# State sums and results inside a chunk as one product, on one core

## The chip, the cores and the metric

The kernel runs on one core of a Trainium2 chip. The metric is the device time of one execution in microseconds. TensorE (PE) multiplies, VectorE (DVE), ScalarE (ACT) and GpSimd (POOL) do the elementwise work, and SyncE (SP) issues nearly all transfers. In the profile PEld stands for the weight loads of TensorE, which run beside its products.

## What is computed

An mLSTM cell over 4 batches x 8 heads, 768 steps, head size 40, and then a SwiGLU block on its 3072 x 320 output with 1536 hidden columns:

```
for t in range(S):
    m_new = maximum(f[t] + m, i[t])
    C = exp(f[t] + m - m_new) * C + exp(i[t] - m_new) * outer(v[t], k[t])
    n = exp(f[t] + m - m_new) * n + exp(i[t] - m_new) * k[t]
    y[t] = sigmoid(o[t]) * (C @ q[t]) / maximum(abs(n @ q[t]), 1)
x = y as (tokens, 320)
out = (silu(x @ w_gate) * (x @ w_val)) @ w_out
```

## The kernel before

**Tiling.** The sequence is cut into six chunks of 128 tokens for all 32 heads, and each chunk into two subchunks of 64 (index i), which lie on partitions 0 to 63 and 64 to 127. Heads are taken in pairs (index two), 16 pairs in all, and the pairs in two groups P of eight (index a). All products are f32. Inside a subchunk the recurrence becomes matrices: scores of keys and queries (`scores`, L309) times exponential weights `w_sb` (`weigh`, L316) give a 64 x 64 matrix per head; its product with the values gives the results inside the subchunk (`intra`, L354). What came earlier is held in a state per subchunk (`C_ring`, three buffers, 41 columns, the last of which carries n), and recalled by a product with the queries (`inter`, L349). The state advances by a decay (POOL, L339) and by the sum of keys times weighted values (`add`, L330; DVE, L341). The weighted values `vw_sb` are made by `weigh_values` (L319).

**On TensorE** each of `scores`, `add`, `inter` and `intra` is 32 matmuls for one group and chunk, 64 rows by 64 columns of stationary operand, issued so that the four follow each other on the four quarters of the array. The profile shows two passes per f32 matmul, each with its own weight load.

**Gathering.** `gather` scales the recalled part (L364), adds the part inside the chunk in four pieces of 64 partitions (L371) and makes the denominator (L373 to L375). `gate` multiplies by the sigmoid of the output gate (L380), `divide` writes `x_sb` (L385), and `seam` transposes it into `xT` (L400), the input of the SwiGLU block.

**The SwiGLU block** for a group g of 512 tokens (128 of each batch) is `hidden(g, m)` for twelve m: 10 matmuls of 64 x 128 stationary and 512 moving columns (L546), Silu on ACT (L551), the product on DVE into `h_sb` (L552); then `project` (L562) or, for group 0, `project_all` (L569).

**Order.** It is written out by hand. While hidden(g, m) runs for group g, the cell work of chunk g + 1 is put between its products by a table of slots, one after each m. The engines run their queues in this order. PSUM has four banks under the tag "cell", handed out in turn to all cell products and transposes, and four under "gen" for the hidden products and the projections. The first chunk is worked ahead of everything, with burns (idle products, L430) between its steps. Meanwhile the weights, which arrive as 64-bit floats, are loaded in pieces (L157) and turned into f32 by `scale` on ACT (L182, L184), `join` on DVE (L192, L193) and `rounded` on POOL or DVE (L200). The stabilizer rows `M_sb` of the later chunks are written to DRAM (L283), and come back spread over 64 partitions as `w_sb` (L408), are subtracted (L412), masked (L417) and exponentiated (L421).

Of the kernel before, what the change touches and what calls it, by code (L numbers as in the profile page):

```python
# [24 lines left out]
def kernel(  # L25
# [55 lines left out]
    def heads(P):  # L81
        return slice(P * UH, (P + 1) * UH)
# [5 lines left out]
    w_sb = const.tile([128, BH, SUB], F32)  # L88
    vw_sb = const.tile([128, BH, D1], F32)
# [23 lines left out]
    def copy(eng, dst, src):  # L113
        if eng is nc.scalar:
            nc.scalar.copy(dst, src)
        else:
            eng.tensor_copy(dst, src)

# [100 lines left out]
    junk = early.tile([128, 512], BF16)  # L219
# [19 lines left out]
    nc.gpsimd.memset(C_ring[0], 0.0)  # L239
# [12 lines left out]
    M_sb = early.tile([BH, NS - 2, SUB], F32)  # L252
# [24 lines left out]
    def late_maxima():  # L277
        nc.vector.tensor_tensor_scan(flat(M_sb), flat(step1), flat(i_sb), M0[0:BH, 1, last], op0=ALU.add, op1=ALU.max)
        nc.vector.tensor_add(m_in[:, 0:1], M0[0:BH, 1:2, last], f0[0:BH, 1:2, last])
        nc.vector.tensor_add(m_in[:, 1:], M_sb[:, 0:NL - 1, last], f_sb[:, 0:NL - 1, last])  # L280
        nc.vector.tensor_sub(step1, m_in.to_broadcast([BH, NL, SUB]), M_sb)
        nc.scalar.activation(step1, step1, AF.Exp)
        nc.sync.dma_start(out=M_dram, in_=flat(M_sb))  # L283

    M_dram = tc.dram_tile([BH, S - L], F32, name="M_dram")
# [27 lines left out]
    def weigh(P, sp):  # L313
        w2 = w_sb[:, heads(P)].rearrange("p (a two) t -> p two a t", two=2)
        for two in range(2):
            nc.vector.tensor_tensor(w2[:, two], sp[two], w2[:, two], op=ALU.mult)  # L316

    def weigh_values(eng, P):
        eng.tensor_tensor(vw_sb[:, heads(P)], v_sb[:, heads(P)], w_sb[:, heads(P), last].to_broadcast([128, UH, D1]),  # L319
                          op=ALU.mult)  # L320
# [3 lines left out]

    def add(P):
        ps = [small("add") for _ in range(2)]
        for a in range(UA):
            for i, two in QUAD:
                h = P * UH + 2 * a + two
                nc.tensor.matmul(ps[i][half(two), a, :], lhsT=k_sb[half(i), h, :], rhs=vw_sb[half(i), h, :],  # L330
                                 start=True, stop=True)
        return ps
# [4 lines left out]
    def next_state(s, P, ps):  # L337
        a = slice(P * UA, (P + 1) * UA)
        nc.gpsimd.tensor_tensor(state(s + 1)[:, a], state(s)[:, a],  # L339
                                dec[:, s - 1, a].unsqueeze(2).to_broadcast([128, UA, D1]), op=ALU.mult)  # L340
        nc.vector.tensor_tensor(state(s + 1)[:, a], state(s + 1)[:, a], ps, op=ALU.add)  # L341


    def attend(n, P):
        inter = [small("inter") for _ in range(2)]
        intra = [small("intra") for _ in range(2)]
        for a in range(UA):
            for two, i in QUAD:
                nc.tensor.matmul(inter[two][half(i), a, :], lhsT=qT[half(two), P * UA + a, half(i)],  # L349
                                 rhs=state(2 * n + i)[half(two), P * UA + a, :], start=True, stop=True)  # L350
        for a in range(UA):
            for i, c in QUAD:
                h = P * UH + 2 * a + (i ^ c)
                nc.tensor.matmul(intra[i][half(c), a, :], lhsT=w_sb[half(i), h, :], rhs=v_sb[half(i), h, :],  # L354
                                 start=True, stop=True)
        return inter, intra

    def gather(n, P, inter, intra):
        y = work.tile([128, UH, D1], F32, name="y_sb")
        y2 = y.rearrange("p (a two) d -> p two a d", two=2)  # L360
        e2 = e_T[:, n, heads(P)].rearrange("p (a two) -> p two a", two=2)
        own = slice(SUB, 128) if n == 0 else slice(0, 128)
        for two in range(2):
            nc.vector.tensor_tensor(y2[own, two], inter[two][own],  # L364
                                    e2[own, two].unsqueeze(2).to_broadcast([own.stop - own.start, UA, D1]), op=ALU.mult)
        for i, c in QUAD:
            t = y2[half(i), i ^ c]
            if n == 0 and i == 0:
                nc.scalar.copy(t, intra[i][half(c)])
            else:  # L370
                nc.vector.tensor_tensor(t, t, intra[i][half(c)], op=ALU.add)  # L371
        den = work.tile([128, UH, 1], F32, name="den")
        nc.vector.scalar_tensor_tensor(den, in0=y[:, :, D:], scalar=-1.0, in1=y[:, :, D:], op0=ALU.mult, op1=ALU.max)  # L373
        nc.vector.tensor_scalar(den, den, scalar1=1.0, scalar2=None, op0=ALU.max)
        nc.vector.reciprocal(den, den)  # L375
        return y, den
# [28 lines left out]
    def weights_load(n):  # L405
        for i in range(2):
            src = M_dram[:, ds((n - 1) * L + i * SUB, SUB)].unsqueeze(0).to_broadcast([SUB, BH, SUB])
            nc.sync.dma_start(out=w_sb[half(i)], in_=src)  # L408

    def weights_sub(n, P):  # L410
        gb = g_T[:, n, heads(P)].unsqueeze(2).to_broadcast([128, UH, SUB])
        nc.vector.tensor_tensor(w_sb[:, heads(P)], gb, w_sb[:, heads(P)], op=ALU.subtract)  # L412

    def weights_mask(P):
        for i in range(2):
            w = w_sb[half(i), heads(P)]
            nc.gpsimd.affine_select(w, w, compare_op=ALU.is_ge, fill=NEG, base=0, pattern=[[0, UH], [1, SUB]],  # L417
                                    channel_multiplier=-1)

    def weights_exp(P):  # L420
        nc.scalar.activation(w_sb[:, heads(P)], w_sb[:, heads(P)], AF.Exp)  # L421
# [5 lines left out]
    def burn(n):  # L427
        t = bank("burn")
        for _ in range(n):
            nc.tensor.matmul(t, lhsT=junk[:, 0:128], rhs=junk, start=True, stop=True)  # L430
# [22 lines left out]
    def first_weights(P):  # L453
        for u in (2 * P, 2 * P + 1):
            nc.scalar.activation(w_sb[:, u * H:(u + 1) * H], wps[u], AF.Exp)
# [3 lines left out]
    def first_sums(P):  # L459
        ps = add(P)  # L460
        for i in range(2):
            nc.scalar.copy(state(i + 1)[:, P * UA:(P + 1) * UA], ps[i])
# [5 lines left out]
    weigh_values(V, 0)  # L468
    sp = scores(0)
    weigh(0, sp)  # L470
    first_sums(0)
# [4 lines left out]
    burn(2)  # L476
    at = attend(0, 0)
    weigh_values(G, 1)
    y0, den0 = gather(0, 0, *at)
# [6 lines left out]
    first_sums(1)  # L486
# [3 lines left out]
    at = attend(0, 1)  # L490
    y1, den1 = gather(0, 1, *at)
# [93 lines left out]
    def do_add():  # L585
        for P in range(2):
            live["add", P] = add(P)

    def do_state(s, P):
        for i, ps in enumerate(live.pop(("add", P))):  # L590
            next_state(s + i, P, ps)

    def do_attend(n, P):
        live["at", P] = attend(n, P)

    def do_gather(n, P, then=True):
        live["y", P] = gather(n, P, *live.pop(("at", P)))
        if then:
            do_gate(P)

    def do_gate(P):
        gate(P, live["y", P][0], nc.gpsimd)

    def do_divide(P):
        divide(P, live.pop(("y", P))[1])

    def load_all(dst, a, n):
        for P in range(2):
# [16 lines left out]
            run(weigh_values, G, 0), run(weigh_values, G, 1), run(piece_load, 8)],  # L625
        9: [run(do_scores), run(do_weigh, 0), run(load_all, o_sb, o_gate, 1)],
        10: [run(do_weigh, 1), run(do_add), run(do_state, 2, 0), run(do_state, 2, 1), run(piece_load, 9)],
        11: [run(do_attend, 1, 0), run(do_gather, 1, 0, False)],
    }
    piece_load(4)  # L630
    for m in range(NFC):
# [4 lines left out]
        0: [run(do_attend, 1, 1), run(convert, 14), run(sig, 0), run(sig, 1), run(do_gate, 0)],  # L636
# [14 lines left out]
    weigh_values(G, 0)  # L651
    weigh_values(G, 1)
# [5 lines left out]
    for g in range(1, NG):  # L658
        n, f = g + 1, g + 2
        slots = {m: [] for m in range(NFC)}  # L660
        if n < NG:
            slots[0] = [run(turn, 0, (A, V), (A, V))]
            slots[1] = [run(turn, 1, (A, V), (A, V))]
            slots[3] = [run(do_scores), run(do_weigh, 0)]
            slots[4] = [run(do_weigh, 1)]
            slots[5] = [run(do_add), run(do_state, 2 * n, 0)]
            slots[6] = [run(do_state, 2 * n, 1)]
            slots[7] = [run(do_attend, n, 0), run(do_gather, n, 0)]
            slots[8] = [run(do_divide, 0)]
            slots[9] = [run(do_attend, n, 1), run(do_gather, n, 1)]  # L670
            slots[10] = [run(do_divide, 1), run(seam, n, 0, (A, V, A, V))]
            slots[11] = [run(seam, n, 1, (A, V, A, V))]
# [9 lines left out]
        for u in range(B):  # L682
# [3 lines left out]
            if f < NG and u == 2:  # L686
                weights_exp(0)
                weights_exp(1)
                sig(0)
                sig(1)  # L690
                weigh_values(nc.gpsimd, 0)
                weigh_values(nc.gpsimd, 1)
# [31 lines left out]
```

## Time and profile before

| | us |
|---|---|
| median of 3 runs | 589.06 (589.0 to 589.62) |
| profiled execution | 589.0, of which the span is 587.2 |
| first hidden product (L546) starts | 45.6 |
| from one group's first hidden product to the next (groups 2, 3, 4) | 90.1 |
| TensorE busy | 564.7 (96% of the span) |
| DVE, ACT, POOL busy | 210.0, 152.0, 101.9 |

The span runs from the first to the last instruction. Up to 45.6 us TensorE is busy for 30.8 us with the first chunk, its transposes and the burns, while the DMA engines are 99% busy. From there to 143 us group 0 runs, with the DMA engines at 89%; from 165 to 506 us TensorE is busy without a gap, and DMA is below a half.

### The profile page before, as it was taken

What the parts mean: (1) busy time and instruction counts of PE and PEld (TensorE: products, weight loads), DVE (VectorE), ACT (ScalarE), POOL (GpSimd) and SP (SyncE); (2) the same over time, 40 slices, a digit from 0 to 9 for tenths busy, and PEclk for the clock granted to TensorE, in tenths of its full rate; (3) what the DMA queues carried; (4) which work ended last, traced back from release to release, by engine and by line L of the source; (5) the groups of instructions that cost most, each with busy time, mean ns of one, the idle gap of its engine ahead of it and who ended that gap; (6) DMA issues with size and microseconds to landing.
All of it is one profiled execution on the core that took longest, in us unless ns stands there. A gap on an engine that the chain in (4) does not pass through costs nothing.

```text
span 587.2 us, 13173 instructions
## 1 busy us (share of the span) xinstructions
PE 564.7 (96%) x5904; PEld 326.2 (56%) x5904; DVE 210.0 (36%) x376; ACT 152.0 (26%) x242; POOL 101.9 (17%) x102
## 2 busy tenths in 40 slices
PE   7759998999999999999999999999999999999997
PEld 4534454676555567555567554567555557544475
DVE  6445666683224630233740223650133550011100
ACT  3437455432601114311014310114211110011100
POOL 2103524455201232001232001133001110000000
PEclk9879999999999999999999999999999999999999
DMA  9999893599304450303360114180000000000000
GB/s 127 180 192 154 169 219 101 129 152 137 55 1 58 80 85 22 57 2 47 61 114 23 35 23 47 32 132 28 18 2 2 2 2 23 22 1 0 1 21 24
DMA packets 129919, 37.91 MB, mean 65 GB/s; under 512 B 120424, under 2 KB 125032, under 8 KB 129864
## 3 DMA queue, kind: packets, MB, share of 16 engines
q1 hardware_dynamic: 129636, 36.85, 36.5%
q8 instruction: 46, 0.75, 0.6%
q10 hardware_dynamic: 228, 0.23, 0.2%
q14 instruction: 9, 0.07, 0.0%
HBM read 33.06 MB, written 4.01 MB: 63 GB/s over the span
## 4 chain that ended last, share of the span: by engine, by line
PE 80%; ACT 1%; DVE 1%; DMA 0%; issue 0%; ACTq 0%; DVEq 0%
PE gv_ps L546 45%; PE o_ps L562 22%; PE o_ps L569 4%; PE inter L349 2%; PE intra L354 2%; PE add L330 2%; PE sp L309 1%; PE tp_kq L294 1%; PE tp_x L400 1%; ACT w_sb L421 0%; DMA out_dram<-z_sb 0%; ACT o_sb L424 0%; ACT L551 0%; ACT L424 0%; ACT L421 0%
## 5 line engine op out<-in xcount | busy, mean ns | idle before, releaser
L546 PE MATMUL gv_ps<-xT,wgv_sb 64*128 64x512 f32 x1440 | 321.7, 594 | 3.6 <-DVE wgv_sb L200 2.6
L546 PEld LDWEIGHTS gv_ps<-xT,wgv_sb 64*128 64x128 f32 x1440 | 138.1, 187 | 158.5 <-issue 151.2
L552 DVE TENSOR_TENSOR h_sb<-sg,gv_ps 128x512 f32<-128x512 f32 x72 | 49.5, 687 | 300.7 <-ACT sg L551 283.8
L562 PE MATMUL o_ps<-wo_sb,h_sb 128*128 128x320 f32 x480 | 130.5, 433 | 0.0
L551 ACT ACTIVATE sg<-gv_ps 128x512 f32<-128x512 f32 x72 | 43.0, 598 | 269.4 <-PE gv_ps L546 269.3
L562 PEld LDWEIGHTS o_ps<-wo_sb,h_sb 128*128 128x128 f32 x480 | 90.8, 190 | 38.2 <-issue 0.8
L339 POOL TENSOR_TENSOR C<-C,dec 128x328 f32<-128x328 f32 x20 | 14.5, 737 | 165.1 <-DVE C L341 165.1
L556 ACT COPY z_sb<-o_ps 128x320 f32<-128x320 f32 x24 | 10.2, 426 | 114.1 <-PE o_ps L562 102.7
L417 POOL TENSOR_SCALAR_AFFINE_SELECT w_sb<-w_sb 64x1024 f32<-64x1024 f32 x20 | 26.8, 1338 | 28.8 <-DVE w_sb L412 27.9
L569 PE MATMUL o_ps<-wo_sb,h_sb 128*128 128x320 f32 x96 | 26.9, 437 | 0.0
L371 DVE TENSOR_TENSOR y_sb<-y_sb,intra 64x328 f32<-64x328 f32 x44 | 21.7, 493 | 7.9 <-PE intra L354 6.9
L380 POOL TENSOR_TENSOR o_sb<-o_sb,y_sb 128x640 f32<-128x640 f32 x10 | 14.2, 1426 | 48.3 <-DVE y_sb L371 48.3
L569 PEld LDWEIGHTS o_ps<-wo_sb,h_sb 128*128 128x128 f32 x96 | 17.9, 190 | 7.2
L319 POOL TENSOR_TENSOR vw_sb<-v_sb,w_sb 128x656 f32<-128x656 f32 x11 | 14.1, 1304 | 39.4 <-issue 29.3
L354 PE MATMUL intra<-v_sb,w_sb 64*64 64x41 f32 x768 | 14.5, 229 | 6.4 <-issue 6.4
L349 PEld LDWEIGHTS inter<-C,qT 64*64 64x64 f32 x768 | 12.5, 134 | 9.0 <-issue 7.8
L330 PEld LDWEIGHTS add<-vw_sb,k_sb 64*64 64x64 f32 x768 | 13.2, 141 | 6.9 <-issue 5.7
L354 PEld LDWEIGHTS intra<-v_sb,w_sb 64*64 64x64 f32 x768 | 13.3, 136 | 6.4 <-issue 6.4
L330 PE MATMUL add<-vw_sb,k_sb 64*64 64x41 f32 x768 | 14.2, 233 | 2.7 <-issue 1.4
L316 DVE TENSOR_TENSOR w_sb<-sp,w_sb 128x512 f32<-128x512 f32 x24 | 15.4, 683 | 2.3 <-PE sp L309 2.2
L200 POOL TENSOR_TENSOR wgv_sb<-both,low 128x640 int32<-128x640 int32 x8 | 12.3, 1542 | 21.3 <-DVE both L193 21.3
L193 DVE SCALAR_TENSOR_TENSOR both<-top,both 128x640 uint32<-128x640 uint32 x18 | 15.7, 870 | 0.6
(111 smaller groups left out, 358.7 us busy)
## 6 DMA issues: line engine op xcount, KB each, us to landing
w_sb<-M_dram SPq DMA_DIRECT2D x10, 512.0 KB, 6.4
k_sb<-in_k_dram SPq DMA_DIRECT2D x12, 320.0 KB, 6.6
q_sb<-in_q_dram SPq DMA_DIRECT2D x12, 320.0 KB, 4.1
v_sb<-in_v_dram SPq DMA_DIRECT2D x12, 320.0 KB, 5.5
o_sb<-in_o_gate_dram SPq DMA_DIRECT2D x12, 320.0 KB, 6.9
raw<-in_moe_w_out_dram SPq DMA_DIRECT2D x3, 1280.0 KB, 6.0
out_dram<-z_sb SPq DMA_DIRECT2D x24, 160.0 KB, 1.8
raw<-in_moe_w_gate_dram SPq DMA_DIRECT2D x3, 640.0 KB, 6.6
```

Source lines behind the costliest of these rows:

```text
L193: nc.vector.scalar_tensor_tensor(both, in0=top, scalar=0x80000000, in1=both, op0=ALU.bitwise_and, op1=ALU.bitwise_or)
L316: nc.vector.tensor_tensor(w2[:, two], sp[two], w2[:, two], op=ALU.mult)
L330: nc.tensor.matmul(ps[i][half(two), a, :], lhsT=k_sb[half(i), h, :], rhs=vw_sb[half(i), h, :], start=True, stop=True)
L349: nc.tensor.matmul(inter[two][half(i), a, :], lhsT=qT[half(two), P * UA + a, half(i)], rhs=state(2 * n + i)[half(two), P * UA + a, :], sta ...
L354: nc.tensor.matmul(intra[i][half(c), a, :], lhsT=w_sb[half(i), h, :], rhs=v_sb[half(i), h, :], start=True, stop=True)
L371: nc.vector.tensor_tensor(t, t, intra[i][half(c)], op=ALU.add)
L417: nc.gpsimd.affine_select(w, w, compare_op=ALU.is_ge, fill=NEG, base=0, pattern=[[0, UH], [1, SUB]], channel_multiplier=-1)
L546: nc.tensor.matmul(ps[i], lhsT=wgv_sb[half(i), PAIRS[kc][i], ts(m, 128)], rhs=x[half(i), kc, :], start=(kc == 0), stop=(kc == NKC - 1))
L551: nc.scalar.activation(sg, ps[0], AF.Silu)
L552: nc.vector.tensor_tensor(hid(g, m), sg, ps[1], op=ALU.mult)
L562: nc.tensor.matmul(p, lhsT=hid(g, m)[:, ts(u, L)], rhs=wo_sb[:, m, :], start=(m == 0), stop=(m == NFC - 1))
L569: nc.tensor.matmul(ps[u], lhsT=hid(g, m)[:, ts(u, L)], rhs=wo_sb[:, m, :], start=(m == 0), stop=(m == NFC - 1))
```

## The change

The weights `w_sb` and new weighted keys `kw_sb` become parts of one tile `wk_sb`, four parts of 64 columns per pair of heads in the order weighted keys 0, weights 0, weights 1, weighted keys 1. `add` now takes two neighbouring parts as one stationary operand of 128 columns, with the plain values as the moving operand; one product gives the state sum of a head on one half of the partitions and its results inside the chunk on the other. The `intra` products go. A product for one group now uses four banks instead of two.

Around it:

- `weigh_keys` takes the place of `weigh_values` (keys of 40 columns instead of values of 41); its zero columns are set once at the start.
- `own_results` copies the results from PSUM into `y_sb`, in four pieces of 64 partitions: on DVE in the first chunk, on ACT later. `next_state` adds in two pieces of 64 partitions per subchunk instead of one of 128.
- `gather` scales the recalled part into the places of `w_sb` that are no longer needed, and adds it to `y_sb` in one operation over 656 columns.
- `recall` leaves out the product with the zero state in chunk 0. In later chunks both groups' recalls stand together in slot 8 (before in slots 7 and 9), with both gathers; `add` of the two groups stands in slots 5 and 6 (before both in 5), the first divide in slot 9. In chunk 1 `add` stands in slots 10 and 11, and both recalls come after the first step of `project_all` (L569).
- `M_dram` is laid out by pairs, so that a row of it holds two heads: the load of `w_sb` has runs of 512 bytes (before 256), the store two transfers with runs of 256 bytes (before one, 2560).
- One call of two burns is left out in the first chunk, `M_sb` shares the buffer of `f_sb`, and the burns' operand is smaller.

```
-    w_sb = const.tile([128, BH, SUB], F32)
-    vw_sb = const.tile([128, BH, D1], F32)
+    wk_sb = const.tile([128, PP, 4, SUB], F32)
...
+    w_sb = wk_sb[:, :, 1:3, :]
+    kw_sb = wk_sb[:, :, 0:4:3, :]
...
+    def weigh_keys(eng, P):
+        eng.tensor_tensor(kw_sb[:, pairs(P), :, 0:D], by_two(k_sb[:, heads(P), 0:D]),
+                          w_sb[:, pairs(P), :, last].to_broadcast([128, UA, 2, D]), op=ALU.mult)
...
     def add(P):
-        ps = [small("add") for _ in range(2)]
-        for a in range(UA):
-            for i, two in QUAD:
-                h = P * UH + 2 * a + two
-                nc.tensor.matmul(ps[i][half(two), a, :], lhsT=k_sb[half(i), h, :], rhs=vw_sb[half(i), h, :],
-                                 start=True, stop=True)
+        ps = [[small("add") for _ in range(2)] for _ in range(2)]
+        for two in range(2):
+            for a in range(UA):
+                for i in range(2):
+                    nc.tensor.matmul(ps[two][i][:, a, :],
+                                     lhsT=wk_sb[half(i), P * UA + a, 2 * two:2 * two + 2, :].rearrange("p x t -> p (x t)"),
+                                     rhs=v_sb[half(i), P * UH + 2 * a + two, :], start=True, stop=True)
         return ps
...
-    def next_state(s, P, ps):
...
+    def next_state(s, P, ps, i):
+        a = pairs(P)
+        new = state(s + 1)
+        nc.gpsimd.tensor_tensor(new[:, a], state(s)[:, a], dec[:, s - 1, a].unsqueeze(2).to_broadcast([128, UA, D1]),
+                                op=ALU.mult)
+        for two in range(2):
+            t = new[half(two), a]
+            nc.vector.tensor_tensor(t, t, ps[two][i][half(two)], op=ALU.add)
+
+    def own_results(ps, engs):
+        y = work.tile([128, UH, D1], F32, name="y_sb")
+        for two in range(2):
+            for i in range(2):
+                copy(engs[i], by_two(y)[half(i), :, two], ps[two][i][half(1 - two)])
+        return y
+
+    def recall(n, P):
...
+                if n or i:
+                    nc.tensor.matmul(inter[two][half(i), a, :], lhsT=qT[half(two), P * UA + a, half(i)],
+                                     rhs=state(2 * n + i)[half(two), P * UA + a, :], start=True, stop=True)
...
+    def gather(n, P, y, inter):
...
+        t = w_sb[own, pairs(P), :, 0:D1]
         for two in range(2):
+            nc.vector.tensor_tensor(t[:, :, two], inter[two][own],
+                                    e2[own, :, two].to_broadcast([own.stop - own.start, UA, D1]), op=ALU.mult)
+        nc.vector.tensor_tensor(by_two(y)[own], by_two(y)[own], t, op=ALU.add)
...
-    burn(2)
-    at = attend(0, 0)
-    weigh_values(G, 1)
-    y0, den0 = gather(0, 0, *at)
+    inter = recall(0, 0)
+    weigh_keys(G, 1)
+    den0 = gather(0, 0, y0, inter)
...
-            slots[5] = [run(do_add), run(do_state, 2 * n, 0)]
-            slots[6] = [run(do_state, 2 * n, 1)]
-            slots[7] = [run(do_attend, n, 0), run(do_gather, n, 0)]
-            slots[8] = [run(do_divide, 0)]
-            slots[9] = [run(do_attend, n, 1), run(do_gather, n, 1)]
+            slots[5] = [run(do_add, 2 * n, 0)]
+            slots[6] = [run(do_add, 2 * n, 1)]
+            slots[8] = [run(do_recall, n), run(do_gather, n, 0), run(do_gather, n, 1)]
+            slots[9] = [run(do_divide, 0)]
```

## The prediction

> **What bounds the kernel now.** I read the busy shares first, then the chain of work that ended last, in order of time, then the weight loads beside it.
>
> ```profile
> PE 564.7 (96%) x5904; PEld 326.2 (56%) x5904; DVE 210.0 (36%) x376; ACT 152.0 (26%) x242; POOL 101.9 (17%) x102
> ...
> PEclk9879999999999999999999999999999999999999
> ```
>
> TensorE is busy 96% of the span, and no other engine half of it. The rest lies in the first slices, where its clock also dips. The chain, for one whole chunk:
>
> ```profile
> 165.05 2.02 PE sp L309 x128
> 167.08 8.78 PE gv_ps L546 x40
> 175.86 2.01 PE add L330 x128
> 177.87 8.78 PE gv_ps L546 x40
> 186.66 1.07 PE inter L349 x64
> 187.73 1.05 PE intra L354 x64
> 188.78 8.78 PE gv_ps L546 x40
> 197.56 1.07 PE inter L349 x64
> 198.64 0.94 PE intra L354 x64
> ...
> 240.18 0.99 PE tp_kq L294 x32
> ```
>
> Start plus duration is the next start: from 165 to 506 us TensorE never waits, so each of its microseconds counts. The profile counts passes: an f32 matmul is two, each with its own weight load. State sums (add) and results inside the chunk (intra) cost 2.01 and 1.05 + 0.94 us per chunk: 4.00. The same products of 64x64 tiles for 64 moving columns (sp) cost no more than for 41, so moving columns are not their limit. Is the weight load? First its groups of instructions by shape (busy us, mean ns of one), then two rows of its timeline (start, duration):
>
> ```profile
> L546 PEld LDWEIGHTS gv_ps<-xT,wgv_sb 64*128 64x128 f32 x1440 | 138.1, 187 | 158.5 <-issue 151.2
> L330 PEld LDWEIGHTS add<-vw_sb,k_sb 64*64 64x64 f32 x768 | 13.2, 141 | 6.9 <-issue 5.7 <-PE sp L309 0.7 <-PE add L330 0.6
> ```
>
> ```profile
> 63.88 0.29 PEld L528 LDWEIGHTS dec_ps<-dec_r,halves 32*128 32x128 f32 x2 [0.76 <-DVE both L192]
> 235.61 0.30 PEld L546 LDWEIGHTS gv_ps<-xT,wgv_sb 64*128 64x128 f32 x4 [0.44 <-issue]
> ```
>
> Two f32 loads of 128 columns one after another last 0.29 us, one alone 0.18: the second starts 0.11 us after the first. Four loads onto two row tiles last 0.30: the two row tiles load at once, and the next pair again 0.11 us later. A load of 64 columns is some 50 ns shorter (141 or less against 187). So f32 weights go in at about 0.85 ns a column.
>
> The start, from TensorE's timeline:
>
> ```profile
> 37.85 0.66 PE L354 MATMUL intra<-v_sb,w_sb 64*64 64x41 f32 x15 [6.38 <-issue]
> ...
> 45.58 13.15 PE L546 MATMUL gv_ps<-xT,wgv_sb 64*128 64x512 f32 x60 [0.99 <-ACT xT L115]
> ```
>
> Inside one product TensorE stands 6.38 us for nothing that the profile shows. Counting passes from the start, its unexplained stops (0.8, 1.8, 1.4 and 6.4 us) fall at passes 348, 475, 602 and 729: one each 127, or some 255 instructions.
>
> [...] 128 add passes on four tiles are 32 rounds, (2.01 - 0.15 for fill) / 32 = 58 ns[...].
>
> **TensorE, part by part (per chunk of 128 tokens).** Removed: add, 128 passes, and intra, 128 passes: 4.00 us. Added: one product of 128 passes (32 matmuls per pair group, two groups), stationary 64x128, on two row tiles: 64 rounds. A round is one 128-column load, 109 ns, and the same few ns over[...]: 113 ns. 64 x 0.113 = 7.2, plus fill of 0.1 twice: 7.4. That half as many instructions are issued doesn't help; the columns loaded per chunk are the same, but two loads run at once instead of four. Recall of both groups in one go keeps its 128 passes, 2.0 us against 1.07 twice, one fill less: -0.1. **Sum +3.3 us per chunk.** Four chunks (165 to 506 us) are wholly on the path: +13.3. The chunk prepared under group 0 (104 to 118 us) gets +3.3, less two waits for weighted scores (0.47 and 0.32 us before add) that the longer first half hides all but 0.3 of: +2.8. No trace row has a short product with such a stationary in ordinary f32. Bounds: below, the transposes' pace, 0.99/32 = 31 ns a pass, if the 109 ns were latency only: 0 per chunk[...]. I take 113, since the pair of loads 0.11 us apart is exactly this shape on these tiles.
>
> **Other engines.** DVE loses 8 adds of 64x328 and 4 state adds of 128x328 (493 ns each), gets 8 state adds of 64x328 and 2 adds of 128x656 (841 by the one DVE row of that size): 5.9 against 5.6. ACT gets 8 copies of 64x328 at 433 ns (L369): +3.5. POOL weighs keys of 128x640 instead of values of 128x656 (1304 ns). All stand under the next hidden product of 4.35 us. On ACT the next Silu queues behind four copies, done 1.9 us after the product; needed at 4.35. One group's product holds all four "cell" banks until ACT's copies, POOL (737), DVE and again POOL and DVE are through, some 4.1 us; the next group wants them at 4.35. Tight: 0, at most 0.5 per chunk. Both gathers in slot 8 keep DVE 5 us ahead of the next h_sb, whose bank is wanted two products on: covered. On SP the v and weight loads of slot 9 wait for gather 1, whose scratch is now w_sb, instead of for intra; they have ten us until used. The weight load is 64 x 16 packets of 512 B per half instead of 64 x 32 of 256 B; the row store becomes 320 packets instead of 32: both off the path.
>
> **The start.** Before, it would have reached L546 at 45.6 - 6.4 = 39.2 without the long stop. After, passes ahead of it fall from 729 and more to 602 (64 intra per group go, recall of the zero state goes)[...]; boundaries now lie in recall 0, in product 1 and at the first hidden pass. On paper: product 0 from 14.4, 3.6 us, to 18.1 (before 15.3); four ACT copies, and the k transposes wait for the third, as the product holds the banks: 19.1; recall 20.5 to 21.5; gather 0.92 + 0.75 + 0.6 and the q copy behind it on DVE: 24.6; scores, weigh, product 1: 30.1; copies 32.1; gate and divide 1.7; gather 2.3; gate and divide 1.7: 37.8; join, rounded, xT copy 3.1: 41. So the longer products cost about 1.8 and the stop gone gives 6.4: **-4.5**. Hidden work of group 0 keeps it: its weights wait on scale 0 and 1 (L182), which come earlier too, and the DMA issues behind them. Bounds: 0, if product 1 meets the lower clock (it fell there before)[...]; -8, if the DVE steps overlap better.
>
> **Sum.** The profiled execution took 589.0 us (span 587.2, 1.8 around it), the median is 589.06. 589.0 + 13.3 + 2.8 - 4.5 = **600.6**.
>
> **The rivals.** (a) The load is not the limit, as above: TensorE unchanged, only the start's gain and 0.5 of waits: 584. For it: transposes with the same 64x128 stationary do 31 ns a pass; against it: their loads are shorter (138 against 187 ns), a cheaper kind. It decides below a round of 77 ns, where five chunks of +1.0 eat the start. 5%. (b) No overlap on two tiles[...]: 616. Against it: 58 ns rounds overlap load and pass. 4%. (c) The start gains nothing, since [...]the clock takes the place of the stop, or the banks of the longer product wait: 605. The likeliest error, 15%. (d) The start gains 8: 597. 10%. An end within 0.2%, by a round near 77 ns: 2%. The main case has the rest, 64%.
>
> **Numbers.** Range 596.5 to 604.5: the start's bounds and 112 to 115 ns a round; (a), (b) and the edge of (c) stay out. A difference of 0.2% (1.2 us) is about what can be told here. Slower 0.93, within 0.2% 0.02, faster 0.05.
>
> **What would show it.** In the chain, add with 64 passes for about 3.7 us twice a chunk, recall of 128 passes for 2.0, no intra; the distance from one group's first hidden product to the next 93.4 us instead of 90.1; first hidden product near 41; PE's passes fewer, its busy time higher. Wrong if 64 passes take 2 us, or if waits on PE for banks or POOL appear behind L546.

## The result and the profile after

The changed kernel took **612.25 us** (median of 4 runs, 611.79 to 614.97) against 589.34 of the kernel before beside it (4 runs, 589.0 to 590.96): a ratio of 1.0393, interval 1.0356 to 1.0429. The sign was forecast, the size not: +22.9 us instead of +11.6. The profiled span is 610.7 us against 587.2, so there are 23.5 us to place. Line numbers below are those of the changed kernel: the hidden product is L559 (before L546), `add` L341 (before L330), `recall` L370 (before `inter`, L349).

The page, busy times, granted clock and the costliest groups (busy us, mean ns of one):

```profile
PE 591.5 (97%) x5070; PEld 354.1 (58%) x5070; DVE 214.0 (35%) x372; ACT 169.5 (28%) x282; POOL 103.1 (17%) x102
...
PEclk9579999899999999999999999899999999999999
...
L559 PEld LDWEIGHTS gv_ps<-xT,wgv_sb 64*128 64x128 f32 x1440 | 140.6, 189 | 160.3 <-issue 151.7
...
L341 PEld LDWEIGHTS add<-v_sb,wk_sb 64*128 64x128 f32 x768 | 48.7, 197 | 7.4 <-issue 6.2
```

TensorE has 834 passes fewer and is busy for 26.8 us more. The loads of `add` were 141 ns each with 64 columns; with 128 they take 197, near the 189 of the hidden product's 128. The clock dips in the first slices, as before, and now also at the eighth and at the 26th. The chain of waits, in order of time, for one whole chunk and for a piece of the next but one:

```profile
269.39 2.02 PE sp L319 x128
271.42 8.78 PE gv_ps L559 x40
280.20 3.50 PE add L341 x64
283.70 4.37 PE gv_ps L559 x20
288.07 3.50 PE add L341 x64
291.57 8.66 PE gv_ps L559 x40
300.23 2.01 PE inter L370 x128
...
380.78 3.50 PE add L341 x64
384.28 10.36 PE gv_ps L559 x40
394.64 2.01 PE inter L370 x128
```

In the steady part the chain is what was forecast: `add` twice with 64 passes, 3.50 us each (3.7 was forecast), recall of 128 passes in 2.01, no `intra`, no gap. A round, one pass on each of two row tiles, is 3.50 / 32 = 109 ns on average. But at 384.28 the same 40 hidden passes take 10.36 us instead of 8.66. What differs in the trace is the clock, 0.50 instead of 1.00 (stretches of the trace: start and end, length, busy time of PE, PEld, DVE, ACT, POOL, each with its count, then the granted clock, DMA share and GB/s):

```profile
114.73:118.14 3.41, 3.41 (x62) 3.35 (x60) 1.35 (x3) 1.46 (x3) 2.24 (x2) 1.00 0.95 366
118.14:121.55 3.41, 3.41 (x13) 2.54 (x12) 1.14 (x3) 2.82 (x5) 0.74 (x1) 0.50 0.01 4
380.97:384.38 3.41, 3.41 (x62) 3.41 (x62) 1.17 (x2) 1.37 (x4) 0.00 (x0) 1.00 0.02 5
384.38:387.79 3.41, 3.41 (x10) 1.39 (x9) 1.49 (x3) 0.79 (x2) 0.73 (x1) 0.50 0.57 96
```

A stretch of 3.41 us in which TensorE does almost nothing but `add` (62 passes in it, never idle) is followed by 3.41 us at half clock, twice. Each costs half of 3.41, 1.7 us, as 10.36 less 8.66 also says. The start, TensorE's timeline:

```profile
14.74 6.16 PE L341 MATMUL add<-v_sb,wk_sb 64*128 64x41 f32 x64 [0.83 <-issue]
...
22.33 1.12 PE L304 MATMUL tp_kq<-ident,k_sb 64*128 64x64 f32 x15 [1.34 <-DVE y_sb L116]
...
23.62 2.28 PE L370 MATMUL inter<-C,qT 64*64 64x41 f32 x32
...
31.31 1.54 PE L341 MATMUL add<-v_sb,wk_sb 64*128 64x41 f32 x24 [0.86 <-DVE wk_sb L326]
33.72 2.43 PE L341 MATMUL add<-v_sb,wk_sb 64*128 64x41 f32 x40 [0.88 <-issue]
...
48.12 1.13 PE L559 MATMUL gv_ps<-xT,wgv_sb 64*128 64x512 f32 x4 [2.32 <-DVE both L201]
```

The unexplained stop of 6.38 us is gone; the longest left is 0.9. Yet the first hidden product starts at 48.1 instead of 45.6: product 0 takes 6.16 us and recall of 32 passes 2.28, and the clock is at 0.50 from 15.7 to 29.4 us. (Of product 0's 6.16 us, 1.00 lie before the fall; half of the other 5.16 added to that is 3.58, an estimate of its time at full clock.) Measured from one group's first hidden product to the next, in the trace:

| part | before | after | difference | forecast |
|---|---|---|---|---|
| start to first hidden product | 45.6 | 48.1 | +2.5 | -4.5 |
| group 0 | 98.4 | 104.4 | +5.9 | +2.8 |
| group 1 | 91.6 | 97.3 | +5.7 | +3.3 |
| group 2 | 90.1 | 92.7 | +2.6 | +3.3 |
| group 3 | 90.1 | 94.4 | +4.3 | +3.3 |
| group 4 | 90.1 | 92.7 | +2.6 | +3.3 |
| group 5 to the end | 81.2 | 81.0 | -0.2 | 0 |

What is in groups 0 and 1? In group 1 TensorE waits for transposed keys, 1.83 us at 164 us where it was 0.38; first the line of the changed kernel, then that of the kernel before:

```profile
164.23 0.27 PE L304 MATMUL tp_kq<-ident,k_sb 64*128 64x64 f32 x1 [1.83 <-ACT kT L114]
```

```profile
154.26 0.27 PE L294 MATMUL tp_kq<-ident,k_sb 64*128 64x64 f32 x1 [0.38 <-ACT kT L115]
```

Behind that are loads of chunk 2, as e3 below shows. SyncE's queue, waits (sum, times, longest) and then its timeline:

```profile
SPq L418 <- DVE y_sb L381: 31.2, 2, 16.4
```

```profile
129.93 1.30 SPq L418 DMA_DIRECT2D wk_sb<-M_dram  x2
...
151.43 4.81 SPq L570 DMA_DIRECT2D out_dram<-z_sb  x4
```

The same two transfers in the kernel before:

```profile
118.33 2.26 SPq L408 DMA_DIRECT2D w_sb<-M_dram  x2
...
142.93 3.25 SPq L557 DMA_DIRECT2D out_dram<-z_sb  x4
```

The load of the weights goes 11.6 us later (9.1 if counted from the first hidden product), because `gather` now uses them as scratch until its last add (L381). All that stands behind it in SyncE's queue goes later too: v, k and q of chunk 2 meet the result stores of group 0.

### The profile page after: what moved, and what is told of

Its sections match the earlier page's. It is cut to its first block, busy times and chain, and to the rows that moved or that the text cites. A ratio compares the mean times of both kernels' runs of the same rounds, so it can differ in the third digit from the quotient of the medians.

```text
span 610.7 us, 11530 instructions
## 1 busy us (share of the span) xinstructions
PE 591.5 (97%) x5070; PEld 354.1 (58%) x5070; DVE 214.0 (35%) x372; ACT 169.5 (28%) x282; POOL 103.1 (17%) x102
## 4 chain that ended last, share of the span: by engine, by line
PE 78%; DVE 3%; ACT 1%; DMA 1%; issue 0%; ACTq 0%; DVEq 0%
PE gv_ps L559 43%; PE o_ps L575 21%; PE add L341 6%; PE o_ps L582 3%; PE inter L370 2%; PE sp L319 1%; PE tp_kq L304 1%; PE tp_x L410 1%; DMA out_dram<-z_sb 1%; DVE both L202 1%; DVE both L201 0%; DVE y_sb L381 0%; ACT wk_sb L431 0%; DVE wk_sb L379 0%; DVE x_sb L395 0%
## 5 line engine op out<-in xcount | busy, mean ns | idle before, releaser
L559 PE MATMUL gv_ps<-xT,wgv_sb 64*128 64x512 f32 x1440 | 324.9, 599 | 4.9 <-DVE wgv_sb L209 2.6
L559 PEld LDWEIGHTS gv_ps<-xT,wgv_sb 64*128 64x128 f32 x1440 | 140.6, 189 | 160.3 <-issue 151.7
L575 PEld LDWEIGHTS o_ps<-wo_sb,h_sb 128*128 128x128 f32 x480 | 90.8, 190 | 38.2 <-issue 0.8
L341 PEld LDWEIGHTS add<-v_sb,wk_sb 64*128 64x128 f32 x768 | 48.7, 197 | 7.4 <-issue 6.2
L341 PE MATMUL add<-v_sb,wk_sb 64*128 64x41 f32 x768 | 48.2, 287 | 2.8 <-issue 1.7
L569 ACT COPY z_sb<-o_ps 128x320 f32<-128x320 f32 x24 | 10.2, 425 | 116.0 <-PE o_ps L575 102.7
L427 POOL TENSOR_SCALAR_AFFINE_SELECT wk_sb<-wk_sb 64x1024 f32<-64x1024 f32 x20 | 27.4, 1368 | 28.5 <-DVE wk_sb L422 27.6
L356 DVE TENSOR_TENSOR C<-C,add 64x328 f32<-64x328 f32 x40 | 19.8, 494 | 31.3 <-ACT y_sb L114 20.4
L114 ACT COPY y_sb<-add 64x328 f32<-64x328 f32 x40 | 17.2, 430 | 22.0 <-PE add L341 21.5
L329 POOL TENSOR_TENSOR wk_sb<-k_sb,wk_sb 128x640 f32<-128x640 f32 x11 | 14.0, 1290 | 36.8 <-DMA out_dram<-z_sb 31.0
L326 DVE TENSOR_TENSOR wk_sb<-sp,wk_sb 128x512 f32<-128x512 f32 x24 | 15.4, 683 | 3.6 <-PE sp L319 3.6
L370 PEld LDWEIGHTS inter<-C,qT 64*64 64x64 f32 x704 | 13.7, 142 | 4.6 <-issue 3.5
L202 DVE SCALAR_TENSOR_TENSOR both<-top,both 128x640 uint32<-128x640 uint32 x18 | 15.7, 871 | 0.6
L319 PEld LDWEIGHTS sp<-qT,kT 64*64 64x64 f32 x768 | 12.4, 135 | 5.6 <-issue 3.9
```

The costliest lines, as they stand in the source:

```text
L202: nc.vector.scalar_tensor_tensor(both, in0=top, scalar=0x80000000, in1=both, op0=ALU.bitwise_and, op1=ALU.bitwise_or)
L319: nc.tensor.matmul(sp[two][half(i), a, :], lhsT=kT[half(two), P * UA + a, half(i)], rhs=qT[half(two), P * UA + a, half(i)], start=True, st ...
L341: nc.tensor.matmul(ps[two][i][:, a, :], lhsT=wk_sb[half(i), P * UA + a, 2 * two:2 * two + 2, :].rearrange("p x t -> p (x t)"), rhs=v_sb[ha ...
L356: nc.vector.tensor_tensor(t, t, ps[two][i][half(two)], op=ALU.add)
L559: nc.tensor.matmul(ps[i], lhsT=wgv_sb[half(i), PAIRS[kc][i], ts(m, 128)], rhs=x[half(i), kc, :], start=(kc == 0), stop=(kc == NKC - 1))
L575: nc.tensor.matmul(p, lhsT=hid(g, m)[:, ts(u, L)], rhs=wo_sb[:, m, :], start=(m == 0), stop=(m == NFC - 1))
```

## The experiments

Ten kernels; e7 and e10 are built on e6, e8 on e3 and e9 on e8. Each first hidden product's start and the distances between groups, in us (the time is one execution for e4 and e5 and a median of 4 or 6 for the others; the kernel before beside them took 589.6 to 590.0; start and distances are those of the profiled execution):

| kernel | time | start | group 0 | 1 | 2 | 3 | 4 |
|---|---|---|---|---|---|---|---|
| before | 589.3 | 45.6 | 98.4 | 91.6 | 90.1 | 90.1 | 90.1 |
| after | 612.3 | 48.1 | 104.4 | 97.3 | 92.7 | 94.4 | 92.7 |
| e1_apart | 599.4 | 50.6 | 101.1 | 94.6 | 90.0 | 90.0 | 90.0 |
| e2_first_apart | 615.6 | 49.8 | 104.5 | 97.3 | 92.7 | 94.4 | 92.7 |
| e3_loads_first | 611.6 | 48.7 | 106.1 | 94.2 | 94.4 | 92.7 | 92.7 |
| e4_twice | 646.3 | 50.8 | 104.4 | 104.4 | 101.3 | 102.9 | 99.6 |
| e5_burn | 616.3 | 48.5 | 107.8 | 97.3 | 94.4 | 92.7 | 92.7 |
| e6_no_zero | 583.1 | 38.4 | 99.5 | 91.6 | 90.3 | 90.1 | 90.1 |
| e7_no_zero_loads | 583.8 | 37.4 | 100.8 | 91.6 | 90.1 | 90.1 | 90.1 |
| e8_halves_loads | 610.0 | 51.2 | 104.4 | 94.2 | 92.7 | 92.7 | 92.7 |
| e9_start_of_before | 600.3 | 38.2 | 108.7 | 94.2 | 92.7 | 92.7 | 92.7 |
| e10_pairs | 583.9 | 37.8 | 101.1 | 91.6 | 90.1 | 90.1 | 90.2 |

The changed kernel, e3, e4 and e8 have the same chunk 0 and start at 48.1, 48.7, 50.8 and 51.2, so a difference of up to 3 us between starts tells nothing by itself. With the chunk 0 of e6, that kernel, e7 and e10 start at 38.4, 37.4 and 37.8.

**e1_apart: the product taken apart, all else as in the change.** Two stationary operands of 64 columns on four tiles in place of one of 128 on two.

```
-                for i in range(2):
-                    nc.tensor.matmul(ps[two][i][:, a, :],
-                                     lhsT=wk_sb[half(i), P * UA + a, 2 * two:2 * two + 2, :]...
+                for i, x in QUAD:
+                    nc.tensor.matmul(ps[two][i][half(x), a, :], lhsT=wk_sb[half(i), P * UA + a, 2 * two + x, :],
```

> The changed kernel with its one product taken apart again: for each head and subchunk two matmuls of 64x64, one for the weights and one for the weighted keys, four tiles in turn; all other edits stay (bank use, copies on ACT, order, loads). My theory (the load of 128 stationary columns on two tiles is what costs, and where such a product fills a 3.4 us stretch the clock falls after it): state sums and results take 1.9 us per pair group instead of 3.5, group to group 90.1 us instead of 92.7; no fall of the clock at 16 us nor in the middle of the kernel; first hidden product at 41 to 43; the wait near 160 us stays; total 586 to 590. Rival (the other edits cost it: copies on ACT, four banks, the order of recall): the total stays above 600 and the start at 48.

599.4 us (598.81 to 599.98), ratio 1.0164 (1.0143 to 1.0185). Its chain, the chunk shown above:

```profile
276.54 2.06 PE add L341 x126
278.60 4.49 PE gv_ps L558 x20
283.10 2.01 PE add L341 x128
285.10 8.78 PE gv_ps L558 x40
293.89 2.01 PE inter L369 x128
```

Twice as many passes take 2.01 us instead of 3.50, and the steady distance is 90.0, that of the kernel before. So the whole +2.6 of a steady group is the shape of the product: 2 x 1.49, less 0.12 twice, since a hidden product (64x128 itself) needs 4.37 after a 64x128 product and 4.49 after one of 64x64. All told the shape is worth 3.3, 2.8, 2.7, 4.4 and 2.7 us in groups 0 to 4, 15.9 together, the clock's falls included. What stays in e1 isn't the shape: 2.7 us in group 0, 2.9 in group 1, and the start (50.6), which lies within the spread above.

**e2_first_apart: the product apart in chunk 0 alone.**

```
-    ps = add(0)
+    ps = add_apart(0)
...
-    ps = add(1)
+    ps = add_apart(1)
```

> The changed kernel with the product taken apart in chunk 0 only. My theory (the start lost its gain because product 0 is slow and leaves TensorE's clock at half from 16 to 30 us): first hidden product at 41 to 43 instead of 48.1, total 606 to 608, group to group 92.7 as before. Rival (the start is late by the four banks, by copies that follow one another on ACT and DVE[...]): first hidden product stays at 47 to 48, total 611 to 613.

615.58 us (614.17 to 616.37), ratio 1.0435 (1.041 to 1.046); the start is at 49.8, no better. In e1 and e2 the 128 passes added bring a long stop back, in the middle of product 1 and at pass 602 in both, 5.40 us in e1 and 5.83 in e2 (in the changed kernel pass 602 is the first hidden product itself). First e1, then e2:

```profile
37.23 1.31 PE L341 MATMUL add<-v_sb,wk_sb 64*64 64x41 f32 x41 [5.40 <-issue]
```

```profile
36.45 1.31 PE L351 MATMUL add<-v_sb,wk_sb 64*64 64x41 f32 x41 [5.83 <-issue]
```

So taking the shape away alone doesn't give the start back.

**e5_burn: four burns more ahead of product 0**, to have the clock up when it comes.

```
     sp = scores(0)
+    burn(4)
```

> The changed kernel with four burns (0.9 us of full products) between the scores and the product of pair group 0 in chunk 0, where TensorE stands idle for 0.9 us. My theory (the clock falls at 16 us[...], and the low clock then stretches product 0 to 6.2 us): the fall comes a stretch or more later, product 0 ends near 18.5 instead of 20.9, first hidden product at 45 to 46.5 instead of 48.1 to 51.1 in the runs so far. Rival (the start is set by copies that follow one another on ACT and DVE[...], whatever the clock): 48 to 51 again.

Start 48.5, 616.32 us in one run. TensorE's timeline:

```profile
16.06 4.36 PE L341 MATMUL add<-v_sb,wk_sb 64*128 64x41 f32 x64
...
31.02 5.55 PE L341 MATMUL add<-v_sb,wk_sb 64*128 64x41 f32 x64 [0.86 <-DVE wk_sb L326]
```

Product 0 does get 1.8 us shorter, but it began 1.3 later, and the half clock falls on product 1 instead (5.55 us). A theory of the clock at product 0 alone fell with this.

**e6_no_zero: the kernel before, with the product with the zero state left out**, the one edit of the change that takes passes away at the start without the new product.

```
+                if n or i:
                     nc.tensor.matmul(inter[two][half(i), a, :], lhsT=qT[half(two), P * UA + a, half(i)],
```

> The kernel before with one part of the change alone: the recall of the zero state in chunk 0 is left out, 64 passes less ahead of the first hidden product. My theory ([...]the late one stops TensorE before pass 729, which now lies behind the results of pair group 1, so that the gather runs during the stop): first hidden product at 40 to 42 instead of 45.6, total 584 to 586. Rival ([...]the stop only moves): first hidden product 45 to 47, total 588 to 591.

583.09 us (582.79 to 583.73), ratio 0.9892 (0.9874 to 0.9911): **faster than both kernels**. TensorE's timeline:

```profile
14.09 1.14 PE L330 MATMUL add<-vw_sb,k_sb 64*64 64x41 f32 x64 [0.45 <-DVE vw_sb L319]
...
23.58 1.09 PE L330 MATMUL add<-vw_sb,k_sb 64*64 64x41 f32 x62
...
28.91 0.48 PE L350 MATMUL inter<-C,qT 64*64 64x41 f32 x9 [2.78 <-issue]
...
38.42 1.99 PE L547 MATMUL gv_ps<-xT,wgv_sb 64*128 64x512 f32 x8
```

The stop of 6.38 us is gone from here too (one of 2.78 is left), the start has 64 passes less, and the first hidden product comes 7.2 us earlier: this is the gain that the prediction booked, and it was there to be had. The changed kernel reaches its first hidden product 9.7 us later than this. At 23.6 us e6 begins the state sums of the second group; the changed kernel begins product 1 at 31.3. e6's clock was full from 13 to 30 us, in the changed kernel it was at half from 15.7 to 29.4.

**e9_start_of_before: the changed kernel with chunk 0 as in the kernel before**, without the zero state, and with the edits of e3 and e8 below in the rest.

```
-    ps = add(0)
-    first_sums(ps, 0)
-    y0 = own_results(ps, (V, V))
+    first_sums0(0)
...
-    inter = recall(0, 0)
-    den0 = gather(0, 0, y0, inter)
+    at = attend0(0)
+    y0, den0 = gather0(0, *at)
```

> Halves and loads first as in the run before last, and chunk 0 as in the kernel before without the recall of the zero state (weighted values, separate products of 64x64, results added from PSUM); the one product only from chunk 1 on. My theory (what is late at the start comes from chunk 0's own product, its copies and the low clock that goes with them, about 10 us against the start without the zero recall, and nothing else of the change touches the start): first hidden product at 38 to 40, total 597 to 600. Rival (the layout of the rows in DRAM, the shared buffers or the copies' place elsewhere make the start late): 45 or later, total over 604.

600.28 us (599.28 to 602.08), ratio 1.0186 (1.0163 to 1.0209). The start is at 38.2, 13.0 earlier than in e8, which differs in chunk 0 alone, and 9.9 earlier than in the changed kernel. So the loss at the start lies in chunk 0's own products, copies, gather and burns. The half clock goes with it in every trace: before the first hidden product it lasts 20.5 to 30.7 us where chunk 0 is that of the change (e1 and e2, with the product apart, among them), and 0.5 to 10.2 us where it is that of before (before, e6, e7, e9, e10). Whether the clock makes the start late or the waits lower the clock isn't shown. But the profiled span is only 8.8 shorter than e8's (600.3 against 609.1): 4.3 us go again in group 0, where the weights of the SwiGLU block are now waited for (3.5 us once, on DVE's conversion) and the clock falls three times.

**e3_loads_first: v, k and q of chunk 2 loaded ahead of the weights**, as they don't need the gather.

```
-        0: [run(do_recall, 1), run(do_gather, 1, 0, False), ...
-        1: [run(do_gather, 1, 1), run(weights_load, 2), run(load_all, v_sb, v, 2)],
+        0: [run(do_recall, 1), run(load_all, v_sb, v, 2), run(load_all, k_sb, k, 2), run(load_all, q_sb, q, 2), ...
+        1: [run(do_gather, 1, 1), run(weights_load, 2)],
...
-        3: [run(do_divide, 1), run(load_all, k_sb, k, 2), run(load_all, q_sb, q, 2), run(load_all, o_sb, o_gate, 2)],
+        3: [run(do_divide, 1), run(load_all, o_sb, o_gate, 2)],
```

> The changed kernel with the loads of values, keys and queries of chunk 2 issued ahead of the load of the weights instead of behind it, so that they don't stand behind its wait for the second gather. My theory (that wait of 16 us pushes the loads of chunk 2 into the writes of group 0's results, ACT's copies wait for these writes, Silu comes late, TensorE waits 1.8 us at 164 and its clock falls at 166): the loads end before 150, that wait falls to 0.4 us and the fall of the clock at 166 goes; first products of groups 1 and 2 are 94 to 95.5 apart instead of 97.4; total 609 to 610.7. Rival (the wait at 164 comes from ACT's queue of exponentials alone): no change, 612.

Group 1 falls from 97.3 to 94.2: the wait of 1.83 us at 164 and the clock's fall that followed it (165.9 us, 1.7) are both gone. So SyncE's order cost 3.1 us there. The total, 611.61 us (607.92 to 614.12), ratio 1.0363 (1.0311 to 1.0416), hardly shows it: in the profiled execution the start is 0.6 and group 0 1.8 us later, and the fall in group 3 has only moved to group 2 (290.5 us).

**e7_no_zero_loads: k and q of chunk 2 loaded ahead of the weights in e6**, v behind them, to see whether the order is good in itself.

```
-        0: [run(do_attend, 1, 1), run(convert, 14), ...
-        1: [run(do_gather, 1, 1), run(weights_load, 2), run(load_all, v_sb, v, 2)],
+        0: [run(do_attend, 1, 1), run(load_all, k_sb, k, 2), run(load_all, q_sb, q, 2), run(convert, 14), ...
+        1: [run(do_gather, 1, 1), run(weights_load, 2)],
...
-        3: [run(do_divide, 1), run(load_all, k_sb, k, 2), run(load_all, q_sb, q, 2), run(load_all, o_sb, o_gate, 2)],
+        3: [run(do_divide, 1), run(load_all, v_sb, v, 2), run(load_all, o_sb, o_gate, 2)],
```

> As the run before (zero recall left out), and keys and queries of chunk 2 are loaded ahead of the weights, the values behind them. My theory (loads of chunk 2 that end earlier leave the writes of group 0's results alone, so that Silu and the transposes of group 1 are not late): 0.4 to 1 us less than without, 583 to 585.5. Rival (in the kernel before those loads end in time already): no difference to the run before.

583.81 us (582.84 to 585.41), ratio 0.991 (0.989 to 0.9931), against 583.09 of e6; group 1 stays at 91.6. So an earlier order of loads gains nothing in a kernel whose gather doesn't hold the weights' load back.

**e4_twice: the second group's product issued twice in chunks 2 to 5**, the second over the first, to price a product and the clock.

```
-        for two in range(2):
+        for two in [0, 1] * times:
```

> The changed kernel with the product of the second pair group issued twice in chunks 2 to 5, into the same banks (the output is the same): 7.0 us on end instead of 3.5. My theory (TensorE's clock falls for a stretch of 3.41 us when the stretch before it is filled by this product[...]): two stretches' length always holds a whole one, so each of the four doubled products is followed by a fall: four falls, each 1.7 us or more, and total 612 + 14 + 7 - 1.7, about 631. Rival (the falls come from waits, or at random): no more falls in the middle than the three of the changed kernel, total 626.

646.28 us in one run. The four groups together are 31.0 us longer than in the changed kernel. Four products more at 3.50 are 14.0. The rest is the clock, which now falls after every doubled product; the first, from 198.2 to 207.1 us, in stretches (columns as above):

```profile
199.80:203.21 3.41, 3.41 (x66) 3.41 (x66) 0.00 (x0) 0.00 (x0) 0.00 (x0) 1.00 0.02 5
203.21:206.62 3.41, 3.41 (x36) 3.41 (x36) 0.49 (x1) 0.87 (x2) 0.00 (x0) 0.50 0.00 0
206.62:210.04 3.42, 3.42 (x14) 1.78 (x14) 1.49 (x3) 0.86 (x2) 0.74 (x1) 0.50 0.60 101
210.04:213.45 3.41, 3.41 (x18) 1.55 (x16) 0.00 (x0) 0.44 (x1) 0.00 (x0) 1.00 0.00 0
```

TensorE is busy in all four; the clock returns at the end of the first stretch that the hidden product nearly fills. In all, 41.0 us of these groups are at half clock, half of which is 20.5; the changed kernel's own two falls there (165.9 and 384.4 us) cost 3.4, so the clock accounts for 17.1, all of the remaining 17.0. The time expected, 631 us, was too low because a doubled product goes on after its fall: the half clock then lasts 6.8 to 10.2 us, where 3.4 was counted.

**e8_halves_loads: e3, with `add` in four halves of 32 passes, each in a slot of its own.** Same matmuls, same number, only apart.

```
-            slots[4] = [run(do_weigh, 1)]
-            slots[5] = [run(do_add, 2 * n, 0)]
-            slots[6] = [run(do_add, 2 * n, 1)]
+            slots[4] = [run(do_weigh, 1), run(do_half, 2 * n, 0, 0)]
+            slots[5] = [run(do_half, 2 * n, 0, 1)]
+            slots[6] = [run(do_half, 2 * n, 1, 0)]
+            slots[7] = [run(do_half, 2 * n, 1, 1)]
```

> The changed kernel with the loads of chunk 2 issued first, and the product of each pair group in chunks 2 to 5 cut into its two halves of 1.8 us, one after each of the hidden products 4 to 7. My theory (only where the product fills most of a 3.41 us stretch does the clock fall): no fall of the clock from 170 us on, each group 92.6 to 93 us after the other, total 605 to 608. Rival (the falls come with any product of this kind, or at random): one or two falls there as in the runs so far, total 609 to 613.

609.99 us (607.23 to 610.87), ratio 1.0339 (1.0313 to 1.0365). From 170 us on the clock does not fall once until the end of the kernel; groups 2, 3 and 4 are all 92.7 (stretches, columns as above):

```profile
170.00:264.00 94.00, 94.00 (x832) 56.92 (x830) 28.97 (x50) 22.80 (x39) 14.34 (x14) 1.00 0.31 50
264.00:356.60 92.60, 92.60 (x826) 55.55 (x824) 28.95 (x50) 22.81 (x39) 14.32 (x14) 1.00 0.30 48
356.60:449.00 92.40, 92.40 (x824) 55.38 (x822) 28.96 (x50) 22.81 (x39) 14.34 (x14) 1.00 0.26 41
```

So the falls in the middle belong to the length of one uninterrupted `add` (e9, with the same halves, has none there either), and the +2.6 of a group does not: it is the rounds of 109 ns.

**e10_pairs: e6 with the rows of the weights stored by pairs**, the change's transfers with runs of 512 bytes, alone.

```
-    M_dram = tc.dram_tile([BH, S - L], F32, name="M_dram")
+    M_dram = tc.dram_tile([PP, NS - 2, 2, SUB], F32, name="M_dram")
...
```

> The kernel before without the recall of the zero state, and one more part of the change alone: the rows in DRAM laid out by pairs, so that the load of the weights has runs of 512 bytes. My theory (the shorter load helps only where the DMA engines are full, up to 100 us, and no product waits for it there): within 0.7 us of the run with the zero recall left out alone, 582.5 to 583.8. Rival (group 0 was slowed by the weights of its later pieces landing behind this load): 581 to 582.4.

583.91 us (582.92 to 584.62), ratio 0.9905 (0.9888 to 0.9921), against 583.09 of e6: no gain, and no loss that can be told. The longer runs are off the path, as forecast.

## Why the prediction was right and wrong

**Right: what bounds, and the sign.** TensorE had no slack from 165 to 506 us, so a product that takes 1.5 us longer shows in full (e1).

**Right in kind, large by a quarter: the load as the limit.** A product was put at 32 rounds of 113 ns and 0.1 us on top, 3.7 us. The 113 can be worked out from the trace of before: 128 columns at its 0.85 ns are 109, and a round of 64 columns took 58, some 4 over the 54 that 64 columns come to. The product took 3.50, which with the same 0.1 on top leaves 106 ns a round, no more than the 109 put for the load alone. So the few ns that the prediction carried over from the 64-column round are not there with 128 columns. And with `add` in the shape of the hidden product 0.12 us go after each product, twice per chunk, which was not counted. +2.6 instead of +3.3 per chunk: over four chunks the forecast was 2.8 us too high, which by luck hid part of the errors below. Rivals (a), no change, and (b), no overlap, are out; the pass time on which (b) put its 616 was the author's and no trace here shows it.

**Right: DVE, ACT and POOL.** The steady groups show no wait on banks, copies or gathers: TensorE's chain is without a gap.

**Failed: "So the longer products cost about 1.8 and the stop gone gives 6.4: -4.5."** The second half held: e6 shows a gain of 7.2 when the stop goes. The first did not. Product 0 was put at 3.6 us and took 6.16; its recall at 1.0 and took 2.28; the k transposes, held by the banks, waited 1.34; product 1 ended at 36.2 instead of 30.1. Against e6 chunk 0 costs 9.7 us more, not 1.8. By place: product 0 takes 5.0 us longer than e6's state sums (6.16 against 1.14); product 1 takes 4.84 with a stop of 0.88 in it, against 1.09, 3.8 longer; the other steps up to its end come to 2.7; and behind it the changed kernel is 1.8 faster, as it has no stop like e6's 2.78. The prediction had the size of product 0 at full clock right (3.58). It named the clock as a bound ("it fell there before") and closed the range at a gain of nothing, without working out what half clock for the whole of product 0 and recall would cost. Rival (c), 605, had the place and the likely causes, but even it took the loss to be no larger than the gain. How the 9.7 divides by cause is open: at full clock each product is some 2.4 us longer than e6's sums and half clock adds 2.6 to product 0, but e5 moved the half clock from product 0 to product 1 and gained nothing, e2 took the shape away and met a long stop again, and what lowers the clock at 15.7 us is not known. Shown is only that it lies in chunk 0's cell work (e9 against e8: 13.0).

**Failed: "Four chunks are wholly on the path: +13.3", at an unchanged clock.** The clock in the middle wasn't considered: it was full there before (1.00 from 165 to 506 us). Two falls follow `add`, one under group 0 (118.1 us) and one under group 3 (384.4), 3.4 us together, and e8 and e1 show that without an `add` of 3.5 us none comes after 170.

**Failed: on SyncE, "they have ten us until used".** The weights' load in group 0 waited 16.4 us, and the k load behind it made TensorE wait 1.45 us longer and dropped the clock once: 3.1 us (e3). The prediction looked at slot 9 of a steady chunk, where the cover is real; the one chunk with another order (slots 0 to 3 of group 0) was not followed through the queue.

**Failed: group 0, "+2.8".** It was 5.9. e1 takes 3.3 of it away: product and clock. Of the 2.7 that stay, some 2.1 are at the seam, the transposition of `x_sb` in two parts of 20 passes: they take 1.40 and 1.45 us, the second after a wait of 0.88, where each took 0.83 without a wait. Both gathers now come after both recalls, behind the first step of the projection, and the chain of waits runs through DVE's gathers there. First the two parts in the changed kernel, then the second in the kernel before:

```profile
133.37 1.40 PE L410 MATMUL tp_x<-ident,x_sb 64*128 64x64 f32 x20
...
137.99 1.45 PE L410 MATMUL tp_x<-ident,x_sb 64*128 64x64 f32 x20 [0.88 <-ACT xT L114]
```

```profile
130.11 0.83 PE L400 MATMUL tp_x<-ident,x_sb 64*128 64x64 f32 x20
```

The sum of the misses: start +7.0, clock after `add` +3.4, loads and their fall +3.1, rest of group 0 +1.4, rounds -2.8, end -0.2: +11.9, which is the 23.5 measured less the 11.6 forecast.

## What to carry over

Here a matmul with few moving columns is priced by its weight columns over the tiles that load at once (128 passes of 64 x 64 take 2.01 us with 41 moving columns and 2.02 with 64): joining two 64-column operands into one of 128 halves the instructions and, on two tiles instead of four, takes the time from 2.01 to 3.50 us. Price an edit's start, middle and odd chunk each by its own order, and follow a tile that is reused as scratch to the loads queued behind it. And try the smallest edit of a bundle alone: here one line, leaving out the product with a zero state, is worth 6 us by itself, and the rest of the change loses 29.

## What the hardware showed that was not expected

**The clock falls while TensorE is busy.** In the changed kernel's trace it falls at 15.74, 36.23, 118.14, 165.93 and 384.38 us, and these lie on a grid: from one to the next are 6, 24, 14 and 64 times 3.413 us. It stays at 0.50 for 13.65, 6.82, 3.41, 3.41 and 3.41 us, whole multiples of the same length. A window below is one such length on this grid. TensorE was busy for all of the 3.41 us ahead of the falls at 118.14 and 384.38, so no idle gap was needed. For each product of `add` in groups 1 to 4 of five kernels (changed, e2, e3, e4, e5; a doubled one counts as one), the largest share of one window that it fills, worked out from the chain's starts and the grid:

| share of one window filled by `add` | products | followed by half clock |
|---|---|---|
| 0.91 to 1.00 | 9 | 9 |
| 0.52 to 0.90 | 31 | 0 |
| at most 0.50 (halves, e8 and e9) | 32 | 0 |

A product of 3.50 us is a little longer than the window, so whether it fills one depends on where it lies: e3's profile has a fall in group 2 where the changed kernel's has one in group 3; its runs lie between 607.9 and 614.1 us, but only one of them has a profile. What it is about `add` that the clock falls after wasn't measured.

Group 0 agrees, in seven kernels (the five above, e8 and e9), counted in TensorE's timeline. There the first product comes in pieces with a wait of 0.21 us between, and its pieces in one window are added up. Each of the eight windows that `add` fills to 0.86 or more is followed by half clock (the one of 0.86 also holds the wait, 0.06 of it), and none that it fills to between 0.30 and 0.80. Four more falls (e3, two in e5, e9) follow windows with no `add` in them, in which TensorE is idle for 0.42 to 0.96 of the time. The falls in chunk 0 aren't separated in this way.

**Stops by a count of passes.** In the kernel before, with the DMA engines 99% busy, one stop comes each 127 f32 passes, 0.8 to 6.4 us long. Pass 602 is a stop in e1, e2, e6, e7, e9 and e10 too, 2.2 to 5.8 us long. Taking 64 passes away gained 7.2 us at the start (e6); with 128 more than the changed kernel, e1 and e2 met stops of 5.4 and 5.8. What makes the stops, and why one is long and another short, isn't shown.
